# A list scheduler's order of instructions, replaced for its first 3391 operations by a written table

## The chip, the core and the metric

The kernel runs on one core of a Trainium2 chip. The metric is the device time of one execution in microseconds (us), the median of several runs. Five engines execute side by side, each in the order in which its instructions were written, and wait for each other on semaphores: TensorE (PE: matmuls; PEld: its weight loads), VectorE (DVE), ScalarE (ACT), GpSimd (POOL) and SyncE (SP), which here issues the DMA transfers.

## What is computed

Attention with a forget gate over 4 x 8 heads of 576 positions, and two feed-forward blocks over the 2304 tokens that come out of it:

```python
scores = (q @ k.transpose(0, 1, 3, 2)) / np.sqrt(64)
cum    = np.cumsum(np.log(np.clip(f, 1e-4, 1.0)), axis=-1)
scores = np.where(causal, -1e9, scores + cum[:, :, :, None] - cum[:, :, None, :])
attn   = softmax(scores)                       # 576 x 576 per head
x = (attn @ v)                                 # to [2304 tokens, 512]
h = x @ w_in1                                  # 512 -> 2048
x = (np.maximum(h, 0) + alpha * np.minimum(h, 0)) @ w_out1
h = x @ w_in2
out = (h * np.tanh(softplus(h))) @ w_out2
```

Everything is float32. The weights arrive as 64-bit floats and are converted on the chip.

## The kernel before

The kernel does not write its instructions in loops. It first records 5138 operations in a `Plan`: each has an engine, a cost, a due time and the operations that it depends on; the 1762 PE operations are small groups of matmuls. A list scheduler (`schedule`) then plays the engines forward in time and takes, on each, the ready operation with the most urgent due time; it does so in ten passes, and the pass with the shortest modelled time gives the order in which `emit` writes all operations. Each engine thus gets its own queue; the semaphores follow from the data. Where an operation needs one of several PSUM banks, the scheduler also chooses the bank.

These are the pieces that the order weaves together (line numbers are those of the profile of before):

- **The start.** POOL and DVE clear tiles; POOL makes the identity matrix `ident`; PE runs 30 matmuls on `ident` (L519) ahead of anything else. The sums of log f are formed on ACT and DVE and sent as rows into the tiles `KM` by SP.
- **Attention, 16 pairs of heads.** Stage M (L616): twelve matmuls of scores a pair, each into one of only three banks, b4, b5 and b6; behind each, DVE takes the row maximum (L623) and so frees the bank. A transposition (L635) brings the maxima into another tile. Stage S (L660): the scores again, transposed, into two pairs of banks, with the exponential on ACT (L670). Stage R (L708): sums of the rows. Stage V (L742): products with v, again into b4 to b6.
- **Feed-forward 1, first part.** Six blocks of 384 tokens go through the first 4 of 16 slices of the hidden width (groups "A", L786 to L788, and "B", L851 to L853). For three of these blocks this is woven into the attention, and all their matmuls go through the single bank b7: a group of twelve matmuls fills it, DVE or ACT reads it (L805 to L814, L323), and only then may the next group begin.
- **Feed-forward 1, the rest, and feed-forward 2.** When the attention has ended, its memory is given to weights; PE then runs groups of L786 to L788 and L851 to L853 in other banks. Meanwhile DVE and ACT convert the weights of feed-forward 2 and SP stores them (`wd<-wb`, L434); SP fetches them back later (`raw<-wd`, L447). Feed-forward 2 follows with L786 to L788 and L862 to L864.

Matmuls come in three shapes of the array: all 128 rows and columns ("r"; all but the following), 64 rows by 128 columns, two side by side ("k": L660), and 128 rows by 64 columns, two side by side ("c": L708 and L742).

Of the kernel before, what the change touches and what calls it, by code (L numbers as in the profile page):

```python
# [18 lines left out]

PRIO = {'': {0: -17.5, 1: -17.2, 2: -11, 3: -11.5, 4: -11.4}, 'A0': {0: -1.0, 1: -1, 2: 7.5, 3: -8.5}, 'A0g': {1: -13.5, 2: -16.5, 3: -21.1}, 'A1': {0: 50, 1: -24.7, 2: 1, 3: -42.4}, 'A1g': {0: -16.6, 1: 5, 2: 6, 3: -0.2}, 'A2': {0: 48.5, 2: -4, 3: 15.2}, 'A2g': {0: 12, 1: -22.0, 2: 30.6, 3: 15}, 'A3': {0: 9.5, 1: -8, 2: -42.3, 3: -28.5}, 'A3g': {0: 31, 1: 4, 2: 54.2, 3: -6}, 'AX': {1: 10.1, 2: 21.5, 3: -5, 4: 12, 5: 11.5, 6: 25.1, 7: 21}, 'B0': {0: 1.3, 1: -1.3, 2: 2, 3: 8, 4: -1}, 'B1': {0: 0.5, 2: -26.9, 3: 2, 4: -17.3}, 'B2': {0: 4.5, 1: 0.5, 2: -31.4, 3: 7.5, 4: 8.5}, 'B3': {0: -15.7, 1: 24, 2: -57.2, 3: 7, 4: 1.5, 5: -3.5, 6: 1.4, 7: 2.5}, 'H0': {0: -1, 1: -0.5, 2: -2.5, 3: -33, 4: 9, 5: 16.5, 6: 11.5, 7: 10}, 'H1': {0: -45.2, 1: -4.5, 2: -40.5, 3: -36.5, 4: -2.5, 5: 4.5, 6: 1, 7: 8, 8: -70.4, 9: -7.1, 10: 3.7, 11: -4, 12: -33.6, 13: -5.5, 14: -30.5}, 'LB2': {0: -1.6, 1: 2, 2: 2, 3: 2}, 'LQ2': {0: -38.9, 1: 20}, 'LV2': {0: 6.3, 1: 20}, 'M2': {0: 20, 1: 6.1, 2: 20, 3: 27.7, 4: 20, 5: 20, 6: 20, 7: -2.4, 8: 20, 9: 21.2, 10: 16.0, 11: 47.1, 12: 20, 13: 30.5, 14: 20, 15: 20, 16: 20, 17: 20, 18: 20, 19: 30.1, 20: 20, 21: 20.5, 22: 20, 23: 20.6}, 'NM2': {0: 0.6, 2: 4.6}, 'O0': {0: -1, 1: -8.5, 2: -11.1, 3: -37, 4: 29.1, 5: 2.5, 6: -0.5, 7: -0.1}, 'O1': {0: -8.5, 1: 22.5, 2: 17.4, 3: 41.2, 4: -9.7, 5: 25, 6: 15.8, 7: 36.5, 8: 62.5}, 'R2': {6: -0.3, 7: -4.9, 9: -1.8, 10: 3.8, 11: -25.5}, 'ST0': {1: 3.2, 3: -4.8}, 'ST1': {0: -6.4, 2: -1.6}, 'ST2': {2: -17.2}, 'ST3': {3: 53.3}, 'T2': {0: -5, 1: -5, 2: -5, 3: -5}, 'W': {0: 36.6, 1: -4, 2: -12.5, 3: -7.6, 4: 34, 5: -33.3, 6: -58.3, 7: 9.5, 8: 30, 9: -6.5, 10: -29.8, 11: -5, 12: 1, 13: -25.9}, 'WA': {0: 2, 1: 4.0, 3: -24.8, 4: -10.5, 5: 6.5, 6: 2, 7: 5, 8: -41.5, 9: -12.9, 10: -6.3, 11: 10.8, 12: 7.5}, 'WF': {0: 33.9, 1: 5.4, 2: -47.5}, 'WS': {0: 1, 1: 4.2, 2: -17, 3: -56, 4: -2, 5: -12.8, 6: -1.4, 7: -6.7, 8: -15.5, 9: -26, 10: -6.8, 11: -40.8, 13: -5.5}, 'X0': {0: -1.6, 1: -52.2, 2: 38.0, 3: -5, 4: -2, 5: 11.5, 6: 22.0, 7: -19.1}, 'X1': {0: -10.8, 1: -14.4, 2: -13.2, 3: -22, 4: -4.5, 5: 16.4, 6: -22.5, 7: -49.3}, 'alph': {0: 60.6, 1: 32.4}, 'const': {0: 46.5, 1: 2}, 'pro2': {1: -42.3, 3: -16.0, 7: -1.2, 8: -7.9, 11: 10.3, 12: 7.7, 13: 19.7, 18: -5.1, 21: -1.9, 22: 17.9, 24: -4.5, 25: 15.7, 26: -9.5, 27: 35.1}, 'warm2': {0: 6.0}}  # L20
ENG = {('A0g', 0): 'ACT', ('A0g', 2): 'ACT', ('A0g', 3): 'POOL', ('A1g', 0): 'ACT', ('A2g', 2): 'ACT', ('A2g', 3): 'DVE', ('A3g', 0): 'DVE', ('AX', 1): 'DVE', ('AX', 2): 'ACT', ('AX', 3): 'DVE', ('AX', 4): 'ACT', ('AX', 5): 'DVE', ('AX', 7): 'DVE', ('B0', 4): 'DVE', ('B3', 4): 'DVE', ('H0', 4): 'ACT', ('H0', 7): 'DVE', ('H1', 13): 'ACT', ('H1', 14): 'DVE', ('NM2', 1): 'ACT', ('NM2', 2): 'ACT', ('O1', 3): 'DVE', ('O1', 5): 'ACT', ('R2', 3): 'POOL', ('T2', 2): 'ACT', ('T2', 3): 'ACT', ('WF', 2): 'DVE', ('X0', 0): 'ACT', ('X0', 1): 'POOL', ('X0', 2): 'ACT', ('X0', 3): 'POOL', ('X0', 4): 'ACT', ('X0', 6): 'ACT', ('X0', 7): 'POOL', ('X1', 0): 'ACT', ('X1', 3): 'POOL', ('X1', 5): 'POOL', ('X1', 6): 'ACT', ('X1', 7): 'POOL'}


class Plan:
# [41 lines left out]
    def add(self, eng, cost, at, fn, r=(), w=(), late=0.0, deps=(), mode="r", port=("POOL",)):  # L66
# [5 lines left out]
        if isinstance(eng, dict):  # L72
            alt, e = eng, ENG.get(key, next(iter(eng)))
            eng, cost, f = e, alt[e], fn
# [95 lines left out]
    def emit(self):  # L170
        ops = self.ops
        N = range(len(ops))
        eng = [o[0] for o in ops]
        dma = [o[5] if o[0] == "SP" else 0.0 for o in ops]

        def graph(found):
            deps = [dict.fromkeys(o[4], True) for o in ops]
            for u, (_, before) in found.items():
                if before is not None:
                    deps[self.uses[u][1][0]].update(dict.fromkeys(self.uses[before][1], True))  # L180
            users = [[] for _ in ops]
            for n in N:
                for d in deps[n]:
                    users[d].append(n)
            return [list(d) for d in deps], users

        def pace(slow):
            cost = [o[1] * (1.0 if o[0] == "PE" else 1.0 + 0.1 * (slow - 1.0)) for o in ops]
            return cost, {e: x * (slow if e != "SP" else (1.0 + slow) / 2) for e, x in self.HOP.items()}

        def total(order, users, slow):

            cost, hop = pace(slow)
            ready, free, queue = [0.0] * len(ops), dict.fromkeys(eng, 0.0), 0.0
            now, door = "", 0.0
            for n in order:
                e = eng[n]
                start[n] = max(free[e], ready[n], door if ops[n][7] else 0.0)
                end = start[n] + cost[n]
                if ops[n][7]:  # L200
                    door = end
                if e == "PE":
                    end += self.SWITCH if ops[n][6] != now else 0.0
                    now = ops[n][6]
                free[e] = end
                if dma[n]:
                    end = queue = max(queue, end + self.DMA_LAG) + dma[n]
                for u in users[n]:
                    ready[u] = max(ready[u], end + (hop[e] if eng[u] != e else self.OWN[e]))
            return max(free.values())  # L210

        cost, hop = pace(1.2)
        start = [0.0] * len(ops)
        prio = [o[2] for o in ops]
        best = None
        deps0, users0 = graph({})
        for _ in range(self.PASSES):
            order, at, found = self.schedule(
                users0, [len(d) for d in deps0], eng, cost, prio,
                lambda a, b: hop[eng[a]] if eng[b] != eng[a] else self.OWN[eng[a]], dma, self.uses)  # L220
            deps, users = graph(found)
            t = sum(total(order, users, x) for x in (1.0, 1.2, 1.6))
            if best is None or t < best[0]:
                best = (t, order, found, users)
            _, back, _ = self.schedule(
                deps, [len(u) for u in users], eng, cost, [-at[n] - cost[n] for n in N],
                lambda a, b: (hop[eng[b]] if eng[a] != eng[b] else self.OWN[eng[b]]) + dma[b] + self.DMA_LAG * (dma[b] > 0), None)
            prio = [-back[n] - cost[n] for n in N]
        _, order, found, users = best
        self.taken = {("use", u): b for u, (b, _) in found.items()}  # L230
        for n in order:
            ops[n][3]()
        self.start = start
        self.total = total(order, users, 1.0)
# [807 lines left out]
```

## Time and profile before

| | us |
|---|---|
| median of 3 runs (1030.51 to 1034.02) | 1030.71 |
| the profiled execution | 1031.08 |
| its span, first to last instruction | 1029.4 |
| PE busy | 1009.9 |
| DVE busy | 746.0 |
| ACT busy | 537.7 |
| POOL busy | 336.7 |

The span is what the trace covers; 1.7 us of the profiled execution lie outside it. A matmul's busy time in the trace overlaps that of the next, so a busy PE may still lose time between the starts of two matmuls: the start-to-start distance tells that.

### The profile page before, as it was taken

The numbers are of one execution on the slowest core, as the hardware profiler recorded it, in microseconds if no ns is written. First come the engines' busy times: TensorE is split into PE (matmuls) and PEld (weight loads), VectorE is DVE, ScalarE is ACT, GpSimd is POOL, SyncE is SP. The second block draws the span as 40 slices with busy tenths as digits, with TensorE's granted clock in tenths as the row PEclk, the third lists the DMA queues.
The fourth block names the chain that finished last, engine by engine and source line by source line (L and its number), as shares of the span: only waits on it lengthen the run. The fifth ranks groups of instructions, "written<-read, shape, count | busy, mean of one in ns | idle before, by whom it ended". The sixth has DMA issues, their size and how long they took to land.

```text
span 1029.4 us, 16893 instructions
## 1 busy us (share of the span) xinstructions
PE 1009.9 (98%) x5996; PEld 909.7 (88%) x5996; DVE 746.0 (72%) x1751; ACT 537.7 (52%) x1127; POOL 336.7 (33%) x351
## 2 busy tenths in 40 slices
PE   7999999999999999999999999999999999999998
PEld 7766777777889999999999999999999999989997
DVE  6587756555498988878642459978698798877975
ACT  4687657654446553534432456555555554555553
POOL 4466535535436330101010111333332332423321
PEclk9999999999999999999999999999999999999999
DMA  5233211210133436575500143000000000000000
GB/s 167 82 106 106 92 52 57 73 49 13 32 100 115 144 116 203 185 238 170 175 1 1 43 112 114 22 1 32 1 11 21 1 31 1 1 32 1 32 1 31
DMA packets 55397, 71.05 MB, mean 69 GB/s; under 512 B 6672, under 2 KB 32272, under 8 KB 55312
## 3 DMA queue, kind: packets, MB, share of 16 engines
q1 hardware_dynamic: 55312, 69.97, 21.6%
q8 instruction: 47, 0.77, 0.3%
q14 instruction: 38, 0.31, 0.1%
HBM read 56.60 MB, written 13.33 MB: 68 GB/s over the span
## 4 chain that ended last, share of the span: by engine, by line
PE 91%; DVE 5%; issue 1%; POOL 1%; ACT 1%; DMA 0%; DVEq 0%; POOLq 0%; ACTq 0%
PE b L786 13%; PE b L787 12%; PE b L788 12%; PE b L864 6%; PE b L863 6%; PE b L862 6%; PE b L851 6%; PE b L853 6%; PE b L660 6%; PE b L852 6%; PE b L742 4%; PE b L616 3%; PE b L519 2%; PE b L708 2%; DVE junk L623 1%
## 5 line engine op out<-in xcount | busy, mean ns | idle before, releaser
L786 PE MATMUL b<-xh,w 128*128 128x384 f32 x768 | 259.0, 337 | 2.3 <-DVE x L323 2.1
L788 PE MATMUL b<-xl,w 128*128 128x384 f32 x768 | 257.4, 335 | 0.0
L787 PE MATMUL b<-xh,w 128*128 128x384 f32 x768 | 257.3, 335 | 0.0
L843 POOL TENSOR_TENSOR x<-x 128x384 f32<-128x384 f32 x96 | 111.6, 1164 | 249.6 <-DVE x L841 193.2
L786 PEld LDWEIGHTS b<-xh,w 128*128 128x128 f32 x768 | 144.2, 188 | 8.7 <-DVE x L323 3.0
L787 PEld LDWEIGHTS b<-xh,w 128*128 128x128 f32 x768 | 144.3, 188 | 3.3 <-POOL w L331 0.3
L788 PEld LDWEIGHTS b<-xl,w 128*128 128x128 f32 x768 | 144.2, 188 | 0.0
L851 PE MATMUL b<-g,w 128*128 128x384 f32 x384 | 130.3, 339 | 1.4 <-DVE x L814 1.2
L853 PE MATMUL b<-g,w 128*128 128x384 f32 x384 | 128.9, 336 | 0.7 <-POOL g L331 0.3
L852 PE MATMUL b<-g,w 128*128 128x384 f32 x384 | 128.4, 334 | 0.0
L321 ACT CAST g<-x 128x384 fp32r<-128x384 f32 x120 | 61.6, 513 | 107.4 <-POOL x L843 55.0
L864 PE MATMUL b<-w,g 128*128 128x512 f32 x288 | 113.2, 393 | 0.0
L863 PE MATMUL b<-w,g 128*128 128x512 f32 x288 | 113.0, 392 | 0.0
L862 PE MATMUL b<-w,g 128*128 128x512 f32 x288 | 112.8, 392 | 0.0
L623 DVE CUSTOM_DVE_ANT_0 junk<-b,tri 128x320 f32<-128x320 f32 (+3 forms) x160 | 69.4, 434 | 49.7 <-PE b L616 37.9
L331 DVE TENSOR_TENSOR g<-x,g 128x384 fp32r<-128x384 f32 x102 | 71.9, 707 | 38.2 <-ACT g L321 37.6
L811 DVE SCALAR_TENSOR_TENSOR X<-X,alph,b 128x384 f32<-128x384 f32 x72 | 43.8, 611 | 56.8 <-ACT X L805 56.5
L805 ACT ACTIVATE X<-b 128x384 f32<-128x384 f32 x72 | 35.3, 490 | 81.1 <-PE b L788 79.5
L331 POOL TENSOR_TENSOR xl<-X,xh 128x384 fp32r<-128x384 f32 x18 | 19.4, 1087 | 174.1 <-ACT xh L321 126.8
L851 PEld LDWEIGHTS b<-g,w 128*128 128x128 f32 x384 | 72.1, 188 | 4.3 <-DVE x L814 1.8
L670 ACT ACTIVATE Pt<-b 128x288 f32<-128x288 f32 (+1 forms) x128 | 56.4, 502 | 37.2 <-PE b L660 36.7
L853 PEld LDWEIGHTS b<-g,w 128*128 128x128 f32 x384 | 72.1, 188 | 1.9 <-DVE g L331 1.3
(93 smaller groups left out, 1941.3 us busy)
## 6 DMA issues: line engine op xcount, KB each, us to landing
raw<-in_moe_w_in_dram SPq DMA_DIRECT2D x64, 256.0 KB
raw<-in_moe_w_out_dram SPq DMA_DIRECT2D x64, 256.0 KB
wd<-wb SPq DMA_DIRECT2D x32, 256.0 KB
raw<-wd SPq DMA_DIRECT2D x32, 256.0 KB
qt<-in_q_dram SPq DMA_DIRECT2D x16, 288.0 KB
kt<-in_k_dram SPq DMA_DIRECT2D x16, 288.0 KB
out_dram<-x SPq DMA_DIRECT2D x18, 256.0 KB
vt<-in_v_dram SPq DMA_DIRECT2D x16, 256.0 KB
```

The lines of the kernel that those rows point to most:

```text
L331: plan.add(engs, 0.0, at, lambda e: (nc.gpsimd if e == "POOL" else nc.vector).tensor_tensor(out=out(), in0=in0(), in1=in1(), op=ALU.subtra ...
L623: nc.vector.tensor_tensor_reduce(out=junk[ql, :z - a], in0=ps()[ql, :z - a], in1=tri[ql, x0 + a:x0 + z], scale=-1.0, scalar=BIG if n == 0 ...
L786: nc.tensor.matmul(ps[:, :NB], w[:, 0, c], xh[c], start=(c == 0), stop=False)
L787: nc.tensor.matmul(ps[:, :NB], w[:, 1, c], xh[c], start=False, stop=False)
L788: nc.tensor.matmul(ps[:, :NB], w[:, 0, c], xl[c], start=False, stop=(c == KC - 1))
L843: add("POOL", c_pool(NB, 2.2), lambda e, m: nc.gpsimd.tensor_tensor(out=m, in0=e, in1=m, op=ALU.mult), [ek, mk], [mk])
L851: nc.tensor.matmul(ps[:, :NB], w[:, 0, c], g[:, 0], start=first, stop=False)
L852: nc.tensor.matmul(ps[:, :NB], w[:, 1, c], g[:, 0], start=False, stop=False)
L853: nc.tensor.matmul(ps[:, :NB], w[:, 0, c], g[:, 1], start=False, stop=last)
L862: nc.tensor.matmul(ps, g[:, 0, sl], w[:, 0], start=first, stop=False)
L863: nc.tensor.matmul(ps, g[:, 0, sl], w[:, 1], start=False, stop=False)
L864: nc.tensor.matmul(ps, g[:, 1, sl], w[:, 0], start=False, stop=last)
```

## The change

The scheduler runs as before and still chooses the banks. After that, its order is thrown away for the operations that a table names: the table lists 3391 operation numbers, and only the operations that it does not name follow behind it in the scheduler's order. The table holds 1122 of the 1762 PE operations: the attention, feed-forward 1 and the first operations of feed-forward 2. By the words of the change the table comes from a local search that begins with the scheduler's own order.

```diff
+ORDER = [int(x) for x in """
+11 29 12 23 15 22 16 17 28 25 14 27 32 5 36 21 35 34 3 31 24 13 33 38 26 89 56 84 9 10 55 113 90 85 18 20 86
...
+3361 2873 3375 3374 3310 3320 3228 3362 3315 3363 3400 2875 2874 3433 3383 3394 3412 3415 3434 3395 3435
+3436 3416 3417 3396 3418 3376 3384 3295 3385 3305 3401 3300 3377 3402 3378 3301 3386
+""".split()]
...
         _, order, found, users = best
+        head = set(ORDER)
+        order = ORDER + [n for n in order if n not in head]
         self.taken = {("use", u): b for u, (b, _) in found.items()}
         for n in order:
             ops[n][3]()
```

No operation, engine, bank or size changes, only the place of operations in the engines' queues. The table moves 935 PE operations by up to 35 places, 630 of ACT, 873 of DVE (by up to 88 places, but for two at the start), 115 of POOL and 271 of SP's 342. On PE the number of times that the shape of the array changes goes from 128 to 148. All lines of the kernel stand 157 lower in the file of the change, so L616 of before is L773 there.

Three places. First POOL at the start of the program, before the change, up to the identity matrix (`masks.py` writes `ident`):

```order
L548 MEMSET KM_1_135 64x576
L546 MEMSET QM_1_131 64x576
L546 MEMSET QM_1_131 3x576
L528 ISA
L528 AFFINE_SELECT tri<-tri 128x128
L550 MEMSET M_142 128x640
L548 MEMSET KM_1_137 64x576
L549 MEMSET BK_138 128x640
L546 MEMSET QM_1_133 64x576
L546 MEMSET QM_1_133 3x576
masks.py:197 MEMSET ident 128x128
masks.py:199 AFFINE_SELECT ident<-ident 128x128
```

One more memory fill, of `Pt` (L531), stands ahead of these. The same queue after the change, from its first row on:

```order
L708 MEMSET vt_145 64x128
L705 MEMSET KM_1_135 64x576
L688 MEMSET Pt_123 32x576
L707 MEMSET M_142 128x640
L705 MEMSET KM_1_137 64x576
masks.py:197 MEMSET ident 128x128
masks.py:199 ISA
masks.py:199 AFFINE_SELECT ident<-ident 128x128
```

The fills of `QM` and `BK` and the mask `tri` have moved behind `ident`, and one small fill of `vt` ahead of it.

Second, PE some 13 us after its first matmul, where the transposition of the first pair's maxima (L635) stands between the score matmuls of the second pair; b4 to b6 are the three banks. Before:

```order
L616 MATMUL b4_69<-KM1_0_136,QM1_0_132 128x320
L616 MATMUL b5_70<-KM1_1_137,QM1_1_133 128x320
L616 MATMUL b6_71<-KM1_0_136,QM1_0_132 128x256
L635 MATMUL b0_65<-ident_73,M50_142 128x128 x3
L635 MATMUL b1_66<-ident_73,M50_142 128x128 x2
L616 MATMUL b4_69<-KM1_1_137,QM1_1_133 128x256
L616 MATMUL b5_70<-KM1_0_136,QM1_0_132 128x64
L616 MATMUL b6_71<-KM1_1_137,QM1_1_133 128x64
L660 MATMUL b2_67<-qt0_124,kt0_127 128x288
```

And after the change:

```order
L773 MATMUL b4_69<-KM1_0_136,QM1_0_132 128x320
L773 MATMUL b5_70<-KM1_1_137,QM1_1_133 128x320
L792 MATMUL b0_65<-ident_73,M50_142 128x128 x3
L792 MATMUL b1_66<-ident_73,M50_142 128x128 x2
L773 MATMUL b4_69<-KM1_1_137,QM1_1_133 128x256
L773 MATMUL b6_71<-KM1_0_136,QM1_0_132 128x256
L773 MATMUL b5_70<-KM1_0_136,QM1_0_132 128x64
L817 MATMUL b2_67<-qt0_124,kt0_127 128x288
```

Before, all six score matmuls of these rows stood ahead of the L660 group; now five do, and the sixth (64 columns) comes two L660 groups later.

Third, PE near the end of the attention, where the last "B" group of the third block ends in b7 and the next "A" group begins there. Before:

```order
L851 MATMUL b7_72<-g3_107,w3_1_87 128x384
L852 MATMUL b7_72<-g3_107,w3_1_87 128x384
L853 MATMUL b7_72<-g3_107,w3_1_87 128x384
L786 MATMUL b7_72<-xh0_96,w3_0_86 128x384
L787 MATMUL b7_72<-xh0_96,w3_0_86 128x384
```

And after:

```order
L1008 MATMUL b7_72<-g3_107,w3_1_87 128x384
L1009 MATMUL b7_72<-g3_107,w3_1_87 128x384
L1010 MATMUL b7_72<-g3_107,w3_1_87 128x384
L899 MATMUL b4_69<-Pt1_123,vt1_146 64x256 x2
L899 MATMUL b4_69<-Pt1_123,vt1_146 64x128 x2
L943 MATMUL b7_72<-xh0_96,w3_0_86 128x384
L944 MATMUL b7_72<-xh0_96,w3_0_86 128x384
```

A product with v (shape c) now lies between the two users of b7.

## Rows read from the trace of the kernel before

**Rows 1.** The page: busy time of each engine, share of the span, instructions.

```profile
PE 1009.9 (98%) x5996; PEld 909.7 (88%) x5996; DVE 746.0 (72%) x1751; ACT 537.7 (52%) x1127; POOL 336.7 (33%) x351
```

**Rows 2.** Stretches: start:end, length, then each engine's busy us, clock, DMA share, GB/s.

```profile
7.00:270.00 263.00, 258.02 (x1964) 198.07 (x1964) 160.13 (x578) 161.73 (x339) 133.13 (x170) 1.00 0.24 73
270.00:325.00 55.00, 51.29 (x288) 49.42 (x287) 47.93 (x98) 28.60 (x66) 26.65 (x22) 1.00 0.29 93
325.00:500.00 175.00, 174.89 (x1005) 173.73 (x1005) 146.14 (x365) 84.38 (x198) 32.30 (x24) 1.00 0.54 173
500.00:640.00 140.00, 140.00 (x807) 139.74 (x807) 73.17 (x135) 59.08 (x119) 13.03 (x12) 1.00 0.22 63
```

**Rows 3.** Waits of PE's weight loads: for whom, us in total, times, longest.

```profile
PEld b L616 <- DVE M L623: 7.8, 22, 0.8
PEld b L786 <- DVE x L323: 3.0, 3, 1.5
PEld b L616 <- DVE nmx L623: 2.5, 8, 0.5
PEld b L851 <- DVE x L814: 1.8, 2, 1.5
PEld b L616 <- DVE X L748: 1.5, 6, 0.5
```

**Rows 4.** Timeline of the start: start us, duration us, instruction, idle time before it.

```profile
0.80 0.57 POOL L531 MEMSET Pt<- 32x576 f32 x1 [0.29 <-POOLq L1019]
3.30 0.62 POOL L550 MEMSET M<- 128x640 f32 x1
6.31 0.19 POOL masks.py:197 MEMSET ident<- 128x128 f32 x1
6.58 0.29 POOL masks.py:199 TENSOR_SCALAR_AFFINE_SELECT ident<-ident 128x128 f32<-128x128 f32 x1
6.92 9.24 PE L519 MATMUL b<-ident 128*128 128x128 f32 x60 [6.92 <-POOL ident masks.py:199]
8.37 0.20 POOL L551 MEMSET vt<- 64x128 f32 x1
10.54 1.63 SPq L579 DMA_DIRECT2D KM<-Pt  x2
15.92 0.39 PE L616 MATMUL b<-KM,QM 128*128 128x320 f32 x1
16.35 0.49 DVE L623 CUSTOM_DVE_ANT_0 junk<-b,tri 128x320 f32<-128x320 f32 x1 [2.74 <-PE b L616]
```

**Rows 5.** Timeline: one wait of a score matmul for its bank.

```profile
29.93 0.30 PE L616 MATMUL b<-KM,QM 128*128 128x64 f32 x1 [0.26 <-DVE nmx L623]
```

**Rows 6.** Timeline of PE: back from shape c at 266.33, out again at 267.57.

```profile
266.33 0.44 PE L851 MATMUL b<-g,w 128*128 128x384 f32 x1
266.61 0.34 PE L852 MATMUL b<-g,w 128*128 128x384 f32 x1
266.78 0.34 PE L853 MATMUL b<-g,w 128*128 128x384 f32 x1
267.31 0.34 PE L853 MATMUL b<-g,w 128*128 128x384 f32 x1
267.57 0.44 PE L708 MATMUL b<-Pt,ones 128*64 128x128 f32 x4
```

**Rows 7.** Timeline: the wait for b7 between two groups.

```profile
269.70 0.34 PE L853 MATMUL b<-g,w 128*128 128x384 f32 x1
270.14 0.56 DVE L323 COPY x<-b 128x384 f32<-128x384 f32 x1 [14.92 <-PE b L853]
270.75 0.44 PE L786 MATMUL b<-xh,w 128*128 128x384 f32 x1 [0.72 <-DVE x L323]
```

**Rows 8.** Timeline of SP: the last store and the fetches of feed-forward 2's weights.

```profile
507.00 0.42 SPq L434 DMA_DIRECT2D wd<-wb  x1
579.44 66.78 SPq L447 DMA_DIRECT2D raw<-wd  x28
```

147 rows, old and new, of the table ORDER are left out of this document.

## The prediction

> **What bounds the kernel now.** First the page: PE is busy for 1009.9 of 1029.4 us and no other engine for more than 746.0 [rows 1]. So the time falls only by what PE loses between its matmuls. Then the stretches: from 325 to 640 us PE idles for 0.11 us in all, from 7 to 270 for 4.98 (263.00 less 258.02), from 270 to 325 for 3.71, and ahead of its first matmul for 6.92 [rows 2, 4]. What can be won lies in the first 325 us.
>
> Idle time is not all of it, since a matmul's busy time covers part of the loss. The waits of PE's weight loads show more: score matmuls (L616) wait for the DVE operation that frees their bank for 7.8 + 2.5 + 1.5 = 11.8 us in 36 waits, and the feed-forward groups (L786, L851) for 3.0 + 1.8 = 4.8 us in five [rows 3]. The reader is to see that these waits are short: none is over 1.5 us, most are near a third of one. They are a matter of what stands between two matmuls in PE's queue.
>
> **The start.** POOL makes `ident` after about 6 us of fills; PE's warm-up block begins at 6.92, runs for 9.00 us, and the first score matmul follows at 15.92 with no wait in its row [rows 4]. So the block and `ident` ahead of it set that moment. In the changed queue POOL does, from 0.80 on, one fill of `vt` (0.20), `KM`, `Pt` and `KM` (576 columns each; 0.57 as the fill of `Pt`), `M` (0.62), then `ident` (0.19 and 0.29): 0.80 + 0.20 + 3 x 0.57 + 0.62 + 0.19 + 0.29 = 3.81 us, and PE follows 0.05 behind, as it does now (6.58 + 0.29 = 6.87 to 6.92) [rows 4]. That is 3.86 instead of 6.92: **-3.1 us**. It holds if the operands of the first score matmul are there at 3.86 + 9.00 = 12.86. The last of them are the rows of `KM`, which SP issues at 10.54 [rows 4]; they hang on a chain of DVE and ACT operations (clip, log, running sum, split) that stands in both queues with about as much work ahead of it. If the rows land after 12.86, the gain shrinks to nothing at 15.92; so the bounds are 0 and -3.1. I take -3.1, because the transfer is some KB and has 2.3 us.
>
> **Score matmuls and their three banks.** A score matmul starts at 15.92, DVE's maximum on it runs from 16.35 to 16.84 [rows 4]: 0.92 us until the bank can be free, plus the way back to PE. A matmul that reuses a bank earlier than that waits; the row at 29.93 is one [rows 5]. I counted, along PE's queue in both orders, the PE work between each of the 192 score matmuls and the next user of its bank, with 0.17 us for a matmul of 384 columns [rows 6], other widths in proportion, and 0.1 for a change of shape. Before, 25 of 192 have less than 0.9 us between them, the shortest 0.06; after, 10, the shortest 0.62. What they lack to 0.9 us adds up to 8.3 us before and 1.7 after; to 1.1 us it is 14.0 and 4.1. The measured 11.8 lies between 8.3 and 14.0, so the count fits, and by it 71 to 80% of the waiting goes: 8.4 to 9.4 us. It leaves out that DVE's own queue is reordered too, and that a maximum which stands behind other work there frees its bank later. I take **-7.5 us**. The bounds are 0 (all of it moved elsewhere) and -11.8.
>
> **The single bank b7 and what follows the attention.** From the last matmul of a group (269.70) to the first of the next (270.75) pass 1.05 us, where 0.17 would do [rows 6, 7]: 0.88 us lost, ended by DVE's copy. The change lays a product with v between these two. Counted as above, 7 of the 23 steps from group to group in the first three blocks have 1.2 us or less between them before, and 3 after. The two longest waits (1.5 us each for L786 and L851 [rows 3]) lie after the attention, where DVE is busy for 47.93 of 55 us [rows 2]; there its queue decides, which my count does not see. I take 0.9 for the wait at 270.75, half of those two (1.5) and half of the rest: **-3 us**, with bounds 0 and -4.8. The view holds further pairs with less than these; I leave them at nothing, and they can give up to 3 us more.
>
> **What it costs: changes of shape.** PE changes the shape of the array 148 times instead of 128. Back from shape c, the second matmul starts 0.28 us after the first, not 0.17; on the way out the next starts 0.26 after, not 0.17 [rows 6]. That is 0.1 us a change, and the first matmul after a return may lose as much again, which no row shows apart. 20 changes cost 2.0 to 4.0 us; I take **+2.6**. The Trainium skill, TensorEngine Tiling (Array Packing), section Tiling Modes, says that a change of the tiling mode, though not of the tile, drains TensorE. It speaks against this change and gives no price. By the rows the sum has +2.6; by a full drain at each it would have more, which is a rival below.
>
> **What costs nothing.** The number and kind of all instructions stay. SP's 271 moved transfers and POOL's later fills (`QM`, `BK`, `tri`) have PE's warm-up block as cover; without it a late `QM` would stop the first score matmuls, at the price named above. In feed-forward 1 the groups are shuffled by up to 35 places among equals, with two to ten us between a producer and its user in both orders; PE has no idle there to win, and the cover is DVE's free time, 29 of 175 us from 325 to 500 and 67 of 140 after [rows 2].
>
> **The sum.** -3.1 - 7.5 - 3 + 2.6 = -11.0 us. Against the profiled execution, 1031.08 us, that is **1020.0 us**. The median of the runs is 0.4 lower, which I leave, since it is less than any term is known to.
>
> **Rivals.**
> - *The waits only move.* PE's queue has more between users of a bank, but DVE's maxima stand behind weight conversions and come later. For it speaks that DVE is reordered as much as PE; against it, that DVE is busy for only 160 of 263 us in the attention [rows 2]. Then start -3.1, banks -2, b7 -1, shapes +2.6: about 1027.5 us, no change that can be told.
> - *The start gives nothing*, since the rows of `KM` or the casts come at 15.9 anyway: 1023 us. It decides if SP issues `KM` later than 10.54.
> - *The shape changes drain the array.* If each new change costs a whole matmul's duration, 0.34 us [rows 6], 20 of them cost 6.8 instead of 2.6: 1024 us. This is what the page's word "drain" would mean here; the rows at 266 and 267 speak against it, since they lose 0.1.
> - *Slower: late stores.* Today the last of 32 weight stores is issued at 507.00 and most fetches of the same weights run from 579 to 646 [rows 8]. In the changed order the last two stores stand among the fetches in SP's queue, with 21 and 4 fetches behind them, and their conversions lie late in DVE's. SP issues in order: a store that waits for DVE holds the fetches behind it. A fetch now takes 66.78 / 28 = 2.4 us [rows 8]; if the first of those two stores comes after feed-forward 2 has begun, some six to eight weights are late one after the other, 15 to 20 us on PE less the gain: about 1036 us. DVE's 67 free us of 140 [rows 2] speak against it.
>
> **How the numbers follow.** The forecast holds 0.62 (gains between 5 and 20 us), waits that only move 0.13, a start without gain 0.08, draining 0.10, late stores 0.07. A measurement of this kernel tells about 0.5%, 5.2 us, from no change. Faster by more: the forecast, the start and the draining cases, 0.80; within: 0.13; slower: 0.07. Range: the best of all terms is -3.1 - 11.8 - 4.8 + 2.0 = -17.7 and up to 3 more from the pairs left out, 1010.4; the poor end is the case of moved waits, 1027.5. I give 1011 to 1028, which leaves out the late stores and the rest of both tails.
>
> **What would show it.** Right: the first warm-up matmul near 3.9 us and the first score matmul near 12.9 with no wait; L616's waits for DVE under 5 us; no wait of L786 near the end of the attention; PE idle from 7 to 270 us below 3 us; feed-forward 2 beginning about 11 us earlier and its own length unchanged. Wrong: a first score matmul that waits for SP or ACT; the same 12 us of bank waits under other lines; start-to-start distances at shape changes of 0.4 us and more; idle of PE between 560 and 660 us released by a weight.

## The result and the profile after

The change ran at a median of 1017.94 us (1017.01 to 1018.63, four runs), the kernel before at 1030.61 (1029.58 to 1034.02, four runs): a ratio of 0.9869, 95% interval 0.9854 to 0.9884. It is faster by 1.3%. The forecast was 1020.0 us with a range of 1011 to 1028.

The profiled execution took 1018.63 us, its span 1016.9. The page's busy line, which answers to [rows 1], and the shares of the chain that ended last:

```profile
PE 1006.0 (99%) x5996; PEld 908.9 (89%) x5996; DVE 742.4 (73%) x1751; ACT 536.0 (53%) x1127; POOL 341.1 (34%) x351
...
PE 97%; DVE 2%; ACT 1%; issue 0%; POOL 0%; DVEq 0%; POOLq 0%; ACTq 0%
```

The instructions are the same in number; PE is busy for nearly the same time, in a span that is 12.5 us shorter. What went is idle time and the short losses between matmuls.

The stretches, laid some 3 us earlier at first and 6 us later on, so that they hold nearly the work of [rows 2]; the columns are the same:

```profile
4.00:264.00 260.00, 257.35 (x1972) 198.29 (x1973) 171.04 (x587) 166.78 (x341) 138.34 (x173) 1.00 0.26 77
264.00:319.00 55.00, 54.29 (x311) 53.51 (x310) 43.66 (x105) 30.03 (x70) 26.94 (x23) 1.00 0.32 98
319.00:494.00 175.00, 175.00 (x1012) 175.00 (x1011) 117.54 (x289) 73.77 (x174) 31.86 (x23) 1.00 0.38 120
494.00:634.00 140.00, 140.00 (x801) 138.91 (x800) 100.06 (x210) 66.28 (x146) 17.34 (x14) 1.00 0.43 134
```

PE's idle time fell from 4.98 to 2.65 us in the first stretch and from 3.71 to 0.71 in the second. In the last one DVE has 100.06 us of work instead of 73.17, and PE still does not wait there: the weight conversions take 30.5 us of it instead of 3.8, so they moved later, into time that was free.

The waits of PE's weight loads, to be read against [rows 3] (L773 is L616 of before, L943 is L786, L1008 is L851):

```profile
PEld b L773 <- DVE M L780: 5.0, 14, 0.8
PEld b L1008 <- DVE x L971: 1.5, 3, 1.0
PEld b L773 <- DVE nmx L780: 1.1, 3, 0.5
PEld b L773 <- DVE wb L562: 0.9, 2, 0.4
PEld b L943 <- DVE x L480: 0.7, 2, 0.5
PEld b L773 <- DVE X L905: 0.2, 1, 0.2
```

The three releasers of the score matmuls in [rows 3] fell from 11.8 us in 36 waits to 6.3 in 18. But new ones appear in small change, the conversions `wb` among them.

The start, which answers to [rows 4]:

```profile
3.45 0.29 POOL masks.py:199 TENSOR_SCALAR_AFFINE_SELECT ident<-ident 128x128 f32<-128x128 f32 x1
3.79 9.44 PE L676 MATMUL b<-ident 128*128 128x128 f32 x60 [3.79 <-POOL ident masks.py:199]
9.71 1.58 SPq L736 DMA_DIRECT2D KM<-Pt  x2
12.99 0.39 PE L773 MATMUL b<-KM,QM 128*128 128x320 f32 x1
```

And the end of the attention on PE, at the place of [rows 7]:

```profile
261.51 0.34 PE L1010 MATMUL b<-g,w 128*128 128x384 f32 x1
261.78 0.87 PE L899 MATMUL b<-Pt,vt 128*64 128x256 f32 x8
262.58 0.44 PE L943 MATMUL b<-xh,w 128*128 128x384 f32 x1
```

The product with v lies between the two users of b7, and L943 starts without a wait.

Where the time was won is read by counting PE's matmul records in both traces and comparing when the same one starts; ahead of the 1800th and of the 2261st stand the same matmuls in both:

| PE's record | before | after | gained up to here |
|---|---|---|---|
| first score matmul | 15.92 | 12.99 | 2.93 |
| the 1800th (attention, near its end) | 247.68 | 240.10 | 7.58 |
| the 2261st (feed-forward 1, last of the third block behind it) | 326.73 | 315.40 | 11.33 |
| first L862 (feed-forward 2) | 636.92 | 624.45 | 12.47 |
| last L864 | 1025.22 | 1012.78 | 12.44 |

So 2.9 us come from the start, 4.7 from the attention, 3.8 from its end and the time just behind it, 1.1 from the rest of feed-forward 1, and nothing from feed-forward 2.

### The profile page after: what moved, and what is told of

Same layout as the page of the kernel before. It is cut to its first block, busy times and chain, and to the rows that moved or that the text cites. A ratio compares the mean times of both kernels' runs of the same rounds, so it can differ in the third digit from the quotient of the medians.

```text
span 1016.9 us, 16752 instructions
## 1 busy us (share of the span) xinstructions
PE 1006.0 (99%) x5996; PEld 908.9 (89%) x5996; DVE 742.4 (73%) x1751; ACT 536.0 (53%) x1127; POOL 341.1 (34%) x351
## 4 chain that ended last, share of the span: by engine, by line
PE 97%; DVE 2%; ACT 1%; issue 0%; POOL 0%; DVEq 0%; POOLq 0%; ACTq 0%
PE b L943 13%; PE b L945 13%; PE b L944 13%; PE b L1008 7%; PE b L1021 7%; PE b L1020 7%; PE b L1019 7%; PE b L1010 6%; PE b L1009 6%; PE b L817 6%; PE b L899 4%; PE b L773 3%; PE b L676 2%; PE b L865 2%; PE b L792 1%; DVE junk L780 1%
## 5 line engine op out<-in xcount | busy, mean ns | idle before, releaser
L943 PE MATMUL b<-xh,w 128*128 128x384 f32 x768 | 258.7, 337 | 0.2 <-DVE x L480 0.2
L944 PE MATMUL b<-xh,w 128*128 128x384 f32 x768 | 257.2, 335 | 0.0
L943 PEld LDWEIGHTS b<-xh,w 128*128 128x128 f32 x768 | 144.2, 188 | 5.3 <-issue 1.2
L944 PEld LDWEIGHTS b<-xh,w 128*128 128x128 f32 x768 | 144.2, 188 | 3.1
L1008 PE MATMUL b<-g,w 128*128 128x384 f32 x384 | 130.1, 339 | 0.8 <-DVE x L971 0.7
L556 ACT ACTIVATE wb<-raw 128x256 f32<-128x256 f32 x128 | 52.9, 433 | 56.4 <-DMA raw<-in_moe_w_out_dram 23.6
L1008 PEld LDWEIGHTS b<-g,w 128*128 128x128 f32 x384 | 72.1, 188 | 3.6 <-DVE x L971 1.5
L558 DVE TENSOR_SCALAR wb<-wb 128x256 int32<-128x256 int32 x128 | 43.8, 357 | 41.0 <-ACT wb L556 40.2
L992 ACT ACTIVATE x<-x,two 128x384 f32<-128x384 f32 x96 | 58.6, 613 | 28.6 <-DVE x L990 28.3
```

The costliest lines, as they stand in the source:

```text
L943: nc.tensor.matmul(ps[:, :NB], w[:, 0, c], xh[c], start=(c == 0), stop=False)
L944: nc.tensor.matmul(ps[:, :NB], w[:, 1, c], xh[c], start=False, stop=False)
L1008: nc.tensor.matmul(ps[:, :NB], w[:, 0, c], g[:, 0], start=first, stop=False)
```

## The experiments

All twelve kernels run the operations of the change or of before; but for the two that add a small matmul, they differ only in order. Lines stand 157 lower than before where nothing else is said.

### The start alone, and all but the start

```diff
+        first = ORDER[:100]
+        order = first + [n for n in order if n not in set(first)]
```

> The order of the change for its first 100 operations (the prologue, the identity matrix, the first loads), the scheduler's order for all others. Theory (the parts add up): the first score matmul comes near 13.0 us as in the change, instead of 15.9, and the end comes 2.9 us earlier than before; about 1027.7 us. Rival (the start's gain is only kept because the later order uses it; with the old order the next wait eats it): the first score matmul comes early, but the end less than 1 us earlier; 1030.

It took 1030.27 us (12 runs, 1028.71 to 1033.81), before 1032.02: 0.9985, interval 0.9974 to 0.9995. The gain, 1.75 us in the medians, lies between the theory's 2.9 and the rival's 1. The counterpart takes the scheduler's first 100 operations and the table behind them:

> The scheduler's order for the first 100 operations, the order of the change for all others. Theory (the parts add up): the first score matmul near 15.9 us, and everything behind it as in the change: about 1020.9 us, 2.9 over the change. Rival (the start does not matter, since something else paces the attention): 1018 to 1019.

It took 1020.69 us (four runs): 0.9890, interval 0.9876 to 0.9904, as the theory had it. Its last L864 starts 10.42 us earlier than before's; the change's 12.44. The difference is 2.0 us, and the start alone gains 1.88 there. Neither is the start's worth as it stands, since the executions differ in one thing more: the warm-up block, with the same matmuls each time, took 9.00 us before, 9.20 in the change, 8.48 in the counterpart and 8.33 with the start alone (see the last section). The order behind it is judged from the first score matmul to the last L864: 1009.31 us before and 1011.22 with the start alone, 999.41 in the counterpart and 999.79 in the change. So of PE's 3.13 us earlier begin 1.9 are lost again in the scheduler's order, and 0.4 in the table's. Part of the loss is seen on PE in the kernel with the start alone:

```profile
12.13 0.39 PE L773 MATMUL b<-KM,QM 128*128 128x320 f32 x1
...
25.39 0.85 PE L773 MATMUL b<-KM,QM 128*128 128x320 f32 x2 [0.49 <-ACT QM L478]
```

PE now comes to the second pair before ACT has cast its `QM`, and waits. An earlier start is worth only as much as the operands behind it also come earlier.

### The order of PE alone, and that of all others

Here one engine (or all but one) has its queue in the change's order and the others theirs as before; where the two contradict each other, the queues that stay near before give way by the least that avoids a deadlock.

```diff
+        queue = {e: [n for n in (full if e in new else order) if eng[n] == e] for e in dict.fromkeys(eng)}
```

> PE's queue word for word as in the change; the queues of ACT, DVE, POOL and SP as before, except for some 80 operations of ACT and 94 of DVE that had to move so that no engine waits for itself. Theory (what is won behind the start is PE work laid between two users of a bank): no gain at the start, since POOL's queue is the old one, but most of the rest: 1021 to 1024 us, with the waits of score matmuls for DVE near those of the change. Rival (the order of DVE and ACT makes the gain, and PE's order without it waits in new places): 1028 us or more, perhaps slower than before.

It took 1155.48 us: 1.1195, interval 1.1180 to 1.1211.

> The queues of DVE, ACT, POOL and SP word for word as in the change; PE's as before, except for some 360 places that had to move. 132 changes of shape on PE instead of 150. Theory (PE's spacing carries what is won behind the start): the start's 2.9 us and little more, about 1025 to 1029 us. Rival (DVE's and ACT's order carries it): 1018 to 1021 us, or less, since the changes of shape are saved.

It took 1234.88 us: 1.1970, interval 1.1950 to 1.1989. With PE's order alone the rival was right in kind; in the other kernel neither held; and both theories were far off in size. The waits of PE's weight loads, first with PE's order alone, then with that of the others (lines 173 lower; L959 is L786, L1024 and L1026 are L851 and L853):

```profile
PEld b L959 <- DVE X L984: 58.7, 22, 7.2
PEld b L959 <- ACT xh L494: 12.1, 5, 9.1
```

```profile
PEld b L1026 <- DVE g L504: 58.4, 31, 9.3
PEld b L1024 <- ACT g L494: 43.0, 17, 7.5
```

Waits of 7 to 9 us, where the longest of [rows 3] was 1.5. Most of it arises in feed-forward 1: PE's 2501st record comes 27 and 46 us later than before, the first L862 125 and 204. I had called that part a shuffle among equals. My reading, which no run tests by itself, is that the groups are equal for PE, but the engine that feeds them makes their operands in another order, and each group waits for an operand that stands some places farther back. Neither kernel tells which engine's order carries the gain, since each mixes two orders that were never fitted to each other. A queue's order can only be judged together with the others'.

### The attention alone, and all but the attention

```diff
+        first = ORDER[:1494]
+        order = first + [n for n in order if n not in set(first)]
```

> The first 1494 operations of the table (the start and the attention), behind them the scheduler's own order: feed-forward 1 after the attention and feed-forward 2 stand as before. My theory: the gain is made ahead of the last quarter of the attention and by the order around its end; the change had won 7.6 us when PE's 1800th matmul began, so this kernel wins that and keeps it, 1021.5 to 1023.5 us. If it wins more than 9.5 us (below 1021), the later 3.8 us come from the attention's own last operations and not from the order behind them. Rival: the part behind pays some of it back, as with the start alone, 1025 us or more.

It took 1023.03 us (four runs): 0.9914, interval 0.9900 to 0.9928, within the theory's bounds. With the scheduler's first 1490 operations and the table's order behind them:

> The scheduler's order for its first 1490 operations (the start and the attention), behind them the table's order. My theory: only what the change won behind the 1800th matmul is left, 12.5 less 7.6, so 4 to 5 us: 1025 to 1027 us. Rival: the two halves depend on each other, and the order behind the attention gives nothing by itself, 1030 us or more.

It took 1027.67 us (five runs): 0.9955, interval 0.9941 to 0.9969. That is 0.7 us above the theory's upper end and 2.3 below the rival's bound; against the kernel before that was timed beside it (1032.01) it is 4.3 us, the 4 to 5 of the theory. In the traces the last L864 comes 7.76 us earlier with the attention alone and 3.76 with the rest alone, 11.5 together of 12.44. Most of the missing 0.9 is the warm-up block again, 9.60 and 9.27 us long in these two. From the first score matmul to the last L864 they take 1004.08 and 1005.28 us, 5.2 and 4.0 less than before; the change takes 9.5 less. So the halves add to within 0.3 us. With the attention alone, PE still stops behind it as it did before:

```profile
271.71 0.45 PE L1010 MATMUL b<-g,w 128*128 128x384 f32 x1 [0.34 <-POOL g L488]
278.09 0.45 PE L943 MATMUL b<-xh,w 128*128 128x384 f32 x1 [1.18 <-DVE x L480]
292.58 0.45 PE L1008 MATMUL b<-g,w 128*128 128x384 f32 x1 [1.19 <-DVE x L971]
...
306.70 2.16 POOL L488 TENSOR_TENSOR xl<-X,xh 128x384 fp32r<-128x384 f32 x2
306.73 1.27 DVE L560 SCALAR_TENSOR_TENSOR wb<-raw,wb 128x256 int32<-128x256 int32 x1
309.17 0.44 PE L1008 MATMUL b<-g,w 128*128 128x384 f32 x1 [0.61 <-DVE x L971]
```

The first three are the two waits of 1.5 us for b7 in [rows 3] and one for `g`. In the change one stop of 0.71 us is left of them. So it is the order behind the attention that removes them. The fourth stop is new; what stands ahead of it, a slow conversion behind a POOL operation, is the subject of the next experiment.

### One operation moved

The kernel before, with the product with v of [rows 7] laid between the two users of b7 (lines 158 lower):

```diff
+        order.remove(1285)
+        order.insert(order.index(1465) + 1, 1285)
```

> The kernel before with one PE operation moved: a product with v (shape c, bank b4, ten matmuls) is laid between the last B group of the third block and the A group that follows it in the single bank b7, where PE lost 0.88 us. My theory: the wait of that A group for DVE's copy goes, and about 0.4 to 0.8 us of start-to-start time with it, since the group that followed the product before now waits a little for it. Rival: the wait only moves to the next user of bank b4, and the gain is below 0.2 us. One look, so read from the trace between 266 and 280 us and not from the time, about 1030 us in either case.

It took 1030.79 us in its one run. The wait is gone: L944 (L786 of before) follows at 269.87, 0.88 us earlier than in [rows 7]. Of this 0.24 were there before: the warm-up block was 0.48 us shorter in this execution, and the 1800th record, ahead of the move, already came 0.24 earlier. So the move won 0.64 us, as the theory had it. But the 2261st record starts only 0.16 us earlier than before's, so all of it is lost again. In between stands a new stop, seen on PE, DVE and POOL:

```profile
314.30 2.18 POOL L489 TENSOR_TENSOR xl<-X,xh 128x384 fp32r<-128x384 f32 x2
314.39 1.23 DVE L561 SCALAR_TENSOR_TENSOR wb<-raw,wb 128x256 int32<-128x256 int32 x1
315.54 0.60 DVE L965 TENSOR_SCALAR x<-b,alph 128x384 f32<-128x384 f32 x1
316.18 0.56 DVE L972 SCALAR_TENSOR_TENSOR x<-b,x 128x384 f32<-128x384 f32 x1
316.79 0.19 PEld L1009 LDWEIGHTS b<-g,w 128*128 128x128 f32 x1 [0.87 <-DVE x L972]
```

DVE's conversion begins 0.09 us behind an operation of POOL and takes 1.23 us; the same line takes 0.42 in the median of its 128 (the view by line has them from 407 to 1797 ns). DVE's reads of the bank stand behind it and come late. In the kernel before, the conversion began 0.02 us ahead of POOL's operation and took 0.41. To test this, the conversion was put behind DVE's next two reads of banks (lines 160 lower):

```diff
+        order.remove(1745)
+        order.insert(order.index(1622) + 1, 1745)
```

> The kernel with the one moved product, and one DVE operation moved besides: the weight conversion that started 0.09 us behind a POOL operation at 314.39 us there and took 1.23 us instead of the usual 0.42, so that DVE's read of bank b7 behind it came late and PE waited 0.72 us at 316.79. It now stands behind DVE's next two reads of banks. My theory: that wait goes, the 0.88 us won at 270 us are kept, and feed-forward 2 starts 0.8 to 1.2 us earlier than in the kernel before (636.92), at 635.7 to 636.1. Rival: the delay moves on to the next conversion or the next read of a bank, and feed-forward 2 starts at 636.4 or later. The times of whole runs scatter by more than this; the start of feed-forward 2 in the trace decides.

It took 1031.09 us (12 runs), before 1031.70: 0.9997, interval 0.9984 to 1.0009. On DVE and POOL now:

```profile
315.26 0.61 DVE L967 TENSOR_SCALAR x<-b,alph 128x384 f32<-128x384 f32 x1
315.30 2.00 POOL L491 TENSOR_TENSOR xl<-X,xh 128x384 fp32r<-128x384 f32 x2
315.90 0.56 DVE L974 SCALAR_TENSOR_TENSOR x<-b,x 128x384 f32<-128x384 f32 x1
```

The stop of PE is gone, so its cause is shown. The saving is not kept: feed-forward 2 starts at 637.21. The warm-up block of that execution took 9.61 us instead of 9.00 (below), 0.61 us that the order does not touch; without it the start would be 636.6, 0.3 us ahead of before, where 0.5 were still ahead at PE's 2261st record. That falls on the rival's side: the rest trickled away in feed-forward 1 in steps that I did not follow.

### The price of a change of shape

One small matmul more in each of the 16 pairs, once among matmuls of its own shape, once in the middle of the row sums (shape c):

```diff
+            nc.tensor.matmul(ps()[1][:, 448:], ident, ident[:, :64], start=True, stop=True)
```

> The kernel of the change with one small matmul more in each of the 16 pairs (identity by 64 of its columns, into columns of the bank that nothing reads), behind the transposition of the maxima, so among matmuls of the same shape of the array: no shape change more. It is the control for the next kernel. My theory: 16 times 0.1 to 0.2 us, so 1.6 to 3.2 us over the change, about 1020 us. Rival: the matmul lies in a time in which PE waits anyway, and costs under 1 us.

> The same 16 small matmuls, each now in the middle of the row sums (shape c), so that the array changes its shape there and back: 32 changes more than in the control. My theory, 0.1 to 0.2 us a change: 3.2 to 6.4 us over the control. Rival, the array drains for a whole matmul, 0.34 us a change: 10.9 us over the control. If it is under 1.5 us, a shape change costs next to nothing and the term of 2.6 us in my sum was too large.

The control took 1019.99 us (0.9888, interval 0.9875 to 0.9902), the other 1025.94 (0.9947, interval 0.9933 to 0.9961). The difference, 5.95 us, is that of 32 changes of shape: 0.19 us each, in the theory's bounds. In the traces, from the first score matmul to the last L864, it is 5.7 us. PE in the control, at the extra matmul (62.52) and at the row sums (67.28), then in the other:

```profile
62.52 0.33 PE L793 MATMUL b<-ident 128*128 128x64 f32 x2
62.66 0.62 PE L773 MATMUL b<-KM,QM 128*128 128x320 f32 x3
...
67.28 0.44 PE L866 MATMUL b<-Pt,ones 128*64 128x128 f32 x4
67.55 0.93 PE L866 MATMUL b<-accp,ones 128*64 128x160 f32 x8
```

```profile
68.87 0.44 PE L865 MATMUL b<-Pt,ones 128*64 128x128 f32 x4
69.24 0.43 PE L867 MATMUL b<-ident 128*128 128x64 f32 x2
69.61 0.98 PE L865 MATMUL b<-accp,ones 128*64 128x160 f32 x8
```

From start to start it is 0.14 + 0.27 us in the control and 0.37 + 0.37 in the other: 0.33 us for two changes, 0.17 each, beside 0.19 from the times.

### What bounds the start now

The change's kernel with `ident` as POOL's first operation (lines 162 lower than before):

```diff
+        order.remove(IDENT)
+        order.insert(0, IDENT)
```

> The kernel of the change with the identity matrix made as POOL's very first operation, so that the warm-up block can begin about 1.5 us instead of 3.8. My theory: the block still sets the first score matmul down to the moment at which the rows of KM have landed and their cast is done; SP issued them at 9.71 and the first score matmul stood at 12.99, so it comes at 11.0 to 12.0 and the time is 1016.0 to 1017.5. Rival: the score matmul already waits for those rows or their casts at 12.9, and the time stays within 0.4 us of the change's, 1018.

It took 1017.39 us (four runs): 0.9860, interval 0.9847 to 0.9874. The time is within the theory's bounds, but the first score matmul came at 12.32, 0.3 us behind them. The block had ended at 10.6; what was late is this:

```profile
7.78 1.67 DVE L563 TENSOR_SCALAR wb<-wb 128x256 int32<-128x256 int32 x2 [0.47 <-ACT wb L561]
9.37 0.73 DVE L700 SCALAR_TENSOR_TENSOR Pt<-Pt 32x576 fp32r<-32x576 f32 x1
10.19 1.57 SPq L741 DMA_DIRECT2D KM<-Pt  x2
12.32 0.38 PE L778 MATMUL b<-KM,QM 128*128 128x320 f32 x1 [1.47 <-DVE wb L567]
```

A weight conversion stands ahead of DVE's last step for the rows of `KM`; SP sends them right behind that step. The releaser in the last row is an early DVE operation; the rows of `KM` are what comes last, since by the trace their transfer has ended at 12.19, and PE begins its weight load at 12.29. So the next kernel puts the whole chain first on its queues (lines 161 lower):

```diff
+START = [5, 11, 9, 10, 89, 56, 84, 55, 113, 22, 12, 23, 15, 16, 52, 51, 17, 18, 53, 54, 20, 19, 29]
```

> The kernel with the identity first, and the other things that the first score matmul needs put first on their queues too: the loads of the first q and k ahead of the weights' on SP, the running sum, the split and their casts ahead of later pairs' fills and of weight conversions on DVE and ACT. With the identity alone first, the block ended near 10.7 us, and the first score matmul waited until 12.3 for the rows of KM, which SP had issued at 10.19 behind DVE's last step at 10.1. My theory: SP issues them at 7.9 to 8.5, they land about 2 us later, the warm-up block sets the first score matmul again, at 10.6 to 11.0, and the time is 1.3 to 1.7 us below that kernel's: 1015.7 to 1016.2. Rival: the weights that now come later cost the first groups in b7 as much, and the time stays at 1017 or above.

```profile
1.42 8.99 PE L680 MATMUL b<-ident 128*128 128x128 f32 x60 [1.42 <-POOL ident masks.py:199]
7.11 0.74 DVE L699 SCALAR_TENSOR_TENSOR Pt<-Pt 32x576 fp32r<-32x576 f32 x1 [0.52 <-ACT Pt L698]
7.94 1.57 SPq L740 DMA_DIRECT2D KM<-Pt  x2
10.16 0.39 PE L777 MATMUL b<-KM,QM 128*128 128x320 f32 x1
```

It took 1016.09 us (four runs): 0.9849, interval 0.9836 to 0.9863. The first score matmul follows the block with no wait, 2.83 us earlier than in the change (0.46 of it because the block was shorter here, 8.74 us instead of 9.20), and the median is 1.3 us below the kernel before this one, at the edge of the theory's 1.3 to 1.7. From the first score matmul to the last L864 it takes 999.55 us, the kernel before this one 999.67, the change 999.79: nothing of the earlier start is given back. It has the lowest median of this study; it was not timed side by side with the change, so only the ratios compare, and their intervals overlap.

## Why the prediction was right, and where its sizes were off

The forecast was -11.0 us against the profiled execution; it was -12.45. The mechanism held: short waits between matmuls went because other work stands between them; one kernel shows it by itself, for the wait at 270.75. By its steps:

- **The start, -3.1.** PE began at 3.79 (forecast 3.86) and the first score matmul at 12.99 with no wait (12.86): -2.93, with a block that took 0.2 us longer. That is what the step said. What it did not say is that a part can be given back later, where later operands are not earlier: 0.4 us in the change's order, 1.9 in the scheduler's, by two experiments.
- **Score matmuls, -7.5.** Mis-sized for the rows it named: 11.8 fell to 6.3 us, -5.5, not below the 5 that I had set as a mark, and with all of its releasers on other engines the line fell from 13.0 to 9.2, -3.7. Other lines took part: behind the start and up to the 1800th record, the listed waits of all lines for other engines fell from 18.5 to 13.2 us. In time the stretch won 4.65 us net, in spite of 18 more changes of shape (137 instead of 119 up to that record, counted in the trace), 3.1 to 3.4 us by the experiment. So 7.7 to 8.1 us were won in it, 5.3 of them in listed waits; where the other 2.4 to 2.8 lie stays open. That the stretch won about what the term said is in part luck: the waits that the term was counted from gave less, and what filled the gap was not in the count.
- **b7 and behind the attention, -3.** Too small. The wait at 270.75 went, as forecast. From there on PE stood still five times before (0.72, 0.34, 1.19, 1.20 and 0.28 us) and once after (0.71). In time it is -3.8 and another -1.1 later. I had summed only the two releasers of [rows 3] and halved what I could not follow; waits of L853 for `g`, 2.0 us, were not in the sum at all.
- **Changes of shape, +2.6.** Counted in the trace there are 150 instead of 132, where this step had 148 instead of 128: 18 more; at 0.17 to 0.19 us each they cost 3.1 to 3.4 us. The bounds of 2.0 to 4.0 held; what I had not been sure of, a loss on the return as well, is real. The rival of 0.34 us each is refuted for shape c, where the price was measured; for the changes between r and k, 84 instead of 76, I take the same price. The Trainium skill, TensorEngine Tiling (Array Packing), section Tiling Modes, speaks of a drain at such a change and gives no price; here it is 0.17 to 0.19 us, half a 384-column matmul's duration.
- **What costs nothing.** True of the change, but not for the reason given. Free time on DVE is no cover when an engine's order changes alone: that cost 123 and 203 us. It cost nothing because all queues moved together.
- **Late stores.** The stores moved as foreseen, but not late enough to do harm: the rival needed the first of the last two behind the beginning of feed-forward 2, at 624.45, and it came at 588.17. SP's queue after the change:

```profile
588.17 0.42 SPq L591 DMA_DIRECT2D wd<-wb  x1
588.68 33.92 SPq L604 DMA_DIRECT2D raw<-wd  x17
622.65 0.42 SPq L591 DMA_DIRECT2D wd<-wb  x1
625.40 8.86 SPq L604 DMA_DIRECT2D raw<-wd  x4
```

The two last stores do lie among the fetches, and a fetch follows the first of them 0.09 us after its end. PE had no idle time from 319 us on.

## What to carry to other kernels

When the busiest engine is at 98% of the span, what is left is short: look at its weight loads' waits, at the distance from one start to the next, and at what could stand between two users of a buffer. Change an order on all engines together, and judge a single move by a milestone far behind it, since all of the 0.6 us won here was lost again 46 us later. Set the warm-up block apart before two single traces are compared. And at the start follow the whole chain to the first useful matmul: moving one link uncovers the next.

## What the runs showed of the hardware

**DVE behind POOL.** The conversion of one 128x256 tile, with two inputs, took 0.42 us in the median and 1.23 us where it began 0.09 us behind the beginning of a POOL operation; it ended 0.28 us behind the end of that operation. This is no single case: in each of the fourteen traces 12 to 17 of the 256 conversions of this kind took over 0.5 us, and every one of these began inside a POOL operation and ended 0.27 to 0.29 us behind its end. DVE's read of a bank at 315.90, in the kernel with the conversion moved, also began inside a POOL operation, and took its usual 0.56 us. The Trainium skill, SBUF — State Buffer, section SBUF: two separate sides, says that DVE operations with two inputs from SBUF and POOL operations that read it hold one pair of ports, each for a whole instruction, and that the one which begins first keeps the other waiting. The rows agree, also in that the same conversion took 0.41 us where it began 0.02 us ahead of POOL's operation.

**The length of the warm-up block.** The same 60 matmul records took from 8.07 to 9.61 us from the first to the score matmul, in executions in which that one did not wait. In a first part they start 0.21 us apart, then 0.11, as at the clock's two levels (1.2 and 2.4 GHz). In each of the fourteen traces the record of the full clock begins within 0.1 us of that step, at 11.73 us before and at 9.02 in the change; ahead of it there is no record, and the view by stretches prints 1.00 there. The step came 2.9 to 6.1 us behind the first matmul, with PE busy all the time and the same matmuls in each. This spread, 1.5 us in the block, is more than some effects measured here.

**Waiting and the clock.** In the kernel with PE's order alone the granted clock was 0.83 in the mean from 480 to 540 us, where PE was busy for 41.68 of 60 us and waited as shown above; so a part of that loss is clock and not waiting. Over the whole trace the clock stood at its lower level for 71.7 us, PE busy in 43.9 of them; 384-column matmuls start 0.32 us apart there and 0.17 elsewhere (medians). At the upper level the same matmuls would take about half, so by this estimate at most 22 of some 123 us are clock. With the order of all others it is 146.9 and 107.4 us, so at most 54 of some 203. Most of the rest is waiting: PE's idle time is 106.6 and 156.0 us, where before it was 15.7.
